# One core's order of work: two constants of a planner, two more split transforms, and one block pair that becomes a Strassen pair

## The chip, the cores and the metric

The kernel runs on one core of one Trainium2 chip. The metric is the time of one execution on the device in microseconds; the kernel before has a median of 857.06 us over three runs (853.89 to 859.17). A lower time is better.

## The reference

A sequence of 2048 rows with 640 channels passes through four layers: a convolution layer, a feed-forward layer, and the same two again. Each adds its result to its input, and each works on a layer-normalised copy of the input.

```
k_shift = 4-tap causal convolution of k over the rows     # per channel
kv      = k_shift * v
y       = causal convolution of kv with ssm_k (2048 taps, per channel)
y       = y + kv * ssm_D
A(x)    = layernorm(x) * y
B(x)    = relu(layernorm(x) @ w1) @ w2                    # 640 -> 1728 -> 640
x = q;  x = x + A(x);  x = x + B(x);  x = x + A(x);  x = x + B(x)
```

The convolution result `y` doesn't depend on `x`, so it is computed once and used in both convolution layers. All tensors are float32.

## The kernel before, in words

The 2048 rows form 8 chunks of 256 rows, each held as two halves of 128. A block (a, l) is the feed-forward layer l (0 or 1) of chunk a, together with the convolution layer ahead of it. Chunks 0 and 1 are worked in half blocks of 128 rows, the others in whole blocks of 256 rows. The order of the blocks is: both layers of chunk 0 by halves, both layers of chunk 1 by halves, then (2,0) (3,0) (2,1) (3,1), (4,0) (5,0) (4,1) (5,1), (6,0) (7,0) (6,1) (7,1).

**Convolution.** The 8 x 5 blocks of 256 rows by 128 channels are grouped in 21 units, listed in `units`. A unit holds one or two blocks; its place in the list is its rank. Ranks 0 to 5 are chunks 0 and 1 (ranks 2 and 5 hold one block); rank 6 is the unit of blocks (2,0) and (3,0), and rank 7 that of (2,1) and (2,2). For each unit, `transform` loads k, v and the long filter, makes kv, and takes both through transform matrices on TensorE: "pg" is the filter's result, "pr" the data's. It spills them to HBM as G and A. `products` multiplies the transforms of all pairs of chunks that meet in a unit's output, on VectorE (L676 to L680, tile `pacc`), and brings the sum back with an inverse transform on TensorE into `pq`.

The matrices of these transforms are float32. A transform is either *whole*, one float32 matmul for each piece, which the trace shows as two records (L592 for pr, L714 for pq), or *split*: the operand is cut into a high part by ScalarE (L720 for the inverse) and a rest by VectorE (L721), both of type float32r, and three matmuls take the place of the one (L403, L404, L405). `FA` and `FU` are the ranks from which forward transforms of the data and inverse transforms are split; units of one block are always whole.

From chunk 4 on, sums are made by *accumulating transfers*: DMAs that POOL's queue issues (L489 for gs, L561 for gt and at), which add a tile of SBUF onto another one. There are 40 of them.

**Feed-forward.** w1 and w2 are cut into 7 pairs of hidden blocks, j = 0 to 6, worked in the order `JS = (0, 1, 2, 3, 6, 4, 5)`. `mm1` makes the hidden values (L1150, L1151, L1153, tiles h and hb: three float16 passes, since activations and weights are split into a high and a low float16 part), ScalarE and VectorE split them again, and `mm2` multiplies with w2 (L1122, L1123, L1125). The last pair (6) is only part filled; its second matmul (L1252) moves half of the partitions, after a copy by ScalarE (tile tb, L1243).

In the last four blocks, `WINO`, the second product goes another way: a pair j is worked by the Strassen-Winograd scheme with seven products (`wprod`) where the plain scheme has eight (`wplain`); both are recorded at L1073. The weight sums that it needs are made by `wcombine` (L860 loads, L865 to L868 VectorE, L878 ScalarE, L879 VectorE), which may start when the last unit's inverse transform is done (`gate`, written at L753). In block (6,0) the pairs `JS[:EARLY]` and pair 6 stay plain.

**The order.** Nothing runs in the order of the program text. Every operation is put on record with its engine, an assumed cost, what it reads and writes, and a priority; the class `Plan` then lays them out by a list scheduler (`order`), counts back from the end how late each may be (`latest`), repeats this up to six times with these times as priorities, and issues the best order found. Each engine, SP's and POOL's queues included, works through its list in that order and waits by semaphores. So an assumed cost changes no instruction; it changes their order on all engines. A transfer is reckoned as done 1.9 us after its issue plus its bytes at the rate `DBW` (310e3 bytes a us) plus 1.1 us, whichever queue issues it.

```
best.ready = end          # in order(): from here on, users of the result may be placed
mm, mm4 = (0.121, 0.113)  # assumed us of one split and one whole float32 matmul, two blocks
```

Of the kernel before, what the change touches and what calls it, by code (L numbers as in the profile page):

```python
# [22 lines left out]
S = 2048  # L23
# [13 lines left out]
NX = 4  # L37
LAG = 3
NSPIN = 50
BM, BK = 1.7, 1.7  # L40
CLS = (0, 1, 2.2, 2, 2.5, 3)
DDP = -6.5
# [7 lines left out]
DBW0, FIRST = 385e3, 45  # L50
STALLS = ((3.5, 1.9), (15.0, 1.3))
LATE_DOWN = 0.0
PASSES, RPE, RBW, RLAT = 6, 0.0, 330e3, 1.9
RENGS = ("PE", "ACT", "DVE", "POOL", "SP")
ENDS = []
# [4 lines left out]

STT = ((0, 0), (0, 2), (0, 4))
FA = 6
FU = 8
FG = 11
SPLIT = (2, 0, 1)
HALVES = 2
# [6 lines left out]
STRAIGHT = ((1, 0),)  # L73
SIGNED_G = ()
WINO = ((6, 0), (7, 0), (6, 1), (7, 1))
EARLY = 2
ONPOOL = ()


# [27 lines left out]
class Plan:  # L107
# [99 lines left out]
    def order(self):  # L207
# [7 lines left out]
        events, dma, n, out = [0.0], 0.0, 0, []  # L215
# [19 lines left out]
        while n < len(self.ops):  # L235
            if not events:
                stuck = [(o.eng, o.seq, [t.name for t in o.new]) for e in engs for o in cand[e]]
                raise RuntimeError(f"no order: {stuck[:12]}")
            now = heapq.heappop(events)
            while events and events[0] <= now:  # L240
                heapq.heappop(events)
            while finish and finish[0][0] <= now:
                _, _, o = heapq.heappop(finish)
                for t in o.tiles:
                    t.left -= 1
                    if not t.left and t.ring is not None:
                        t.ring.free += 1
                for d in o.outs:
                    if d.eng == "PE" != o.eng and LATE(d):
                        heapq.heappush(later, (now + LATE(d), d.seq, d))  # L250
                        heapq.heappush(events, now + LATE(d))
                        continue
                    if d.eng == "PE" == o.eng:
                        continue
                    d.left -= 1
                    if not d.left:
                        cand[d.eng].append(d)
            while later and later[0][0] <= now:
                _, _, d = heapq.heappop(later)
                d.left -= 1  # L260
                if not d.left:
                    cand["PE"].append(d)
            for e in engs:
                if free[e] > now + 1e-9:
                    continue
                if e == "SP" and dma > now + LAG:
                    heapq.heappush(events, dma - LAG)
                    continue
                best = None
                rooms = [(max(map(when, o.deps)) - now + SLACK, o.prio) for o in soon.get(e, ()) if o.left]  # L270
                for o in cand[e]:
                    if best is not None and o.prio > best.prio:
                        continue
                    if any(o.cost > room and o.prio > prio for room, prio in rooms):
                        continue
                    if fits(o):
                        best = o
                if best is None:
                    continue
                cand[e].remove(best)  # L280
                for t in best.new:
                    t.ring.free -= 1
                    t.ring.lines[t.stream].pop(0)
                best.start = now
                free[e] = now + best.cost
                end = free[e] + (PEOUT if e == "PE" else 0.08)
                while best.nbytes and stalls and now >= stalls[0][0]:
                    dma = max(dma, now + DLAT) + stalls.pop(0)[1]
                if best.nbytes:
                    dma = max(dma, now + DLAT) + best.nbytes / (DBW0 if now < FIRST else DBW)  # L290
                    end = dma + 1.1
                best.ready = end
                if best.prio[0] == CRIT and e in soon:
                    soon[e].remove(best)
                if e == "PE":
                    for d in best.outs:
                        if d.eng == e:
                            d.left -= 1
                            if not d.left:
                                cand[e].append(d)  # L300
                heapq.heappush(finish, (end, best.seq, best))
                heapq.heappush(events, end)
                heapq.heappush(events, free[e])
                out.append(best)
                n += 1
# [12 lines left out]
def tile_h3_mlp(ctx: ExitStack, tc: tile.TileContext, q, kT, vT, shk, hF, hR, dD, w1, w2, cM, cG, out):  # L318
    nc = tc.nc
    PE, ACT, DVE, POOL, SP = nc.tensor, nc.scalar, nc.vector, nc.gpsimd, nc.sync  # L320
# [19 lines left out]
    def pe(cost, fn, reads, writes, prio, late=0.0):  # L340
        plan.op("PE", cost, fn, reads, writes, prio, late=late)
# [33 lines left out]
    down = keep(const, [P, P], "down", F16)  # L375
    POOL.memset(down.t, 0.0)
    POOL.tensor_copy(down[64:P, 0:64], ident16[64:P, 64:P])
    tb = keep(const, [P, 2 * P], "tb", F16)
# [57 lines left out]
    def transform(u):  # L436
# [6 lines left out]
        n, nm = len(u), "%d_%d" % u[0]  # L443
        pr_ = (CRIT, CONV, LATER)[min(u[0][0], 2)]
        w, h = 2 * n * P, n * P
        mm, mm4 = (0.121, 0.113) if n == 2 else (0.213, 0.063)
        full = n == 1 or rank(u) < FA
        ld = []
        c0 = u[-1][0] == 0
# [2 lines left out]
        for k, src, wd in (("kt", kT, 262), ("vt", vT, 256), ("hf", hF, 256), ("hr", hR, 256))[: 3 if c0 else 4]:  # L452
# [3 lines left out]
            x = R(k, [P, n, wd], k + nm)  # L456
# [61 lines left out]
        if c0 or straight or u[0] in SIGNED_G:  # L518
            srcs = [hf, hr] if straight else [hf]
            for b in range(2):  # L520
                for ri in range(2):
                    for k, x in enumerate(srcs if c0 or straight else gs[ri : ri + 1]):
                        x, xv = x if isinstance(x, tuple) else (x, lambda x=x: hv(x))
# [109 lines left out]
    def products(u, at, gt, after):  # L633
        n, nm = len(u), "%d_%d" % u[0]
        pr_ = (CRIT, CONV, LATER)[min(u[0][0], 2)]
        w, h = 2 * n * P, n * P
        mm, mm4 = (0.121, 0.113) if n == 2 else (0.213, 0.063)
        full = n == 1 or rank(u) < FU
        acc = T(cv, "pacc", 1, [P, n, 768], "pacc" + nm)
        if after:  # L640
# [46 lines left out]
        for ri in range(2):  # L687
            f = T(cv, "u", 2, [P, n, 256], f"u{ri}" + nm)
# [88 lines left out]
    WSRC, WT = {}, {}  # L777
# [246 lines left out]
    def main(n, a, layer, S, xTS):  # L1024
        xT, xS = xTS
        first_ = n == 0
        R = P * len(S)
        x0 = (S[0] - xS[0]) * P
        flat = list({id(x): x for x in xT.values()}.values())
# [99 lines left out]
        def mm1(j, i, p):  # L1129
            tail = j == NFP - 1 and i == 1  # L1130
            z = slice(0, R) if tail else slice(i * R, i * R + R)
            if n == 0 and j == JS[0]:

                def f(x):
                    for t in range(NDT):
                        b, e = t == 0, t == NDT - 1
                        wh, wl = w1at(j, t, i, 0), w1at(j, t, i, 1)
                        PE.matmul(p[:, z], wh, xv(t, x), start=b and x == 0, stop=e and x == 1)
                        if not x:
                            PE.matmul(p[:, z], wl, xv(t, 0), start=False, stop=False)  # L1140

                for x in range(2):
                    pe((10 - 5 * x) * 0.0545 * len(S), lambda x=x: f(x), [xT[0, x], WT[j, 0, 0], WT[j, 0, 1]], [p], FILL)
                return

            def f():
                for t in range(NDT):
                    b, e = t == 0, t == NDT - 1
                    wh, wl = w1at(j, t, i, 0), w1at(j, t, i, 1)
                    PE.matmul(p[:, z], wh, xv(t, 0), start=b, stop=False)  # L1150
                    PE.matmul(p[:, z], wh, xv(t, 1), start=False, stop=tail and e)  # L1151
                    if not tail:
                        PE.matmul(p[:, z], wl, xv(t, 0), start=False, stop=e)  # L1153

            pe((10 if tail else 15) * 0.0545 * len(S), f, [*flat, WT[j, 0, 0], WT[j, 0, 1]], [p], FILL)

        def second(j, *x):
            if len(x) == 4:
# [51 lines left out]
        for j in JS:  # L1210
            p = T(ps, "h", 2, [P, 2 * R], f"h{n}_{j}", stream=sm)
# [8 lines left out]
            p1 = T(ps, "h", 2, [P, 2 * R], f"hb{n}", stream=sm) if j == NFP - 1 else p  # L1220
# [28 lines left out]
                mm2(prev[0], 0, *prev[1:])  # L1249
                mm2(prev[0], 1, *prev[1:])  # L1250
            if j == NFP - 1:
                pe(0.0545 * len(S), lambda p1=p1: PE.matmul(p1[:, 0:R], down.t, tb[:, 0:R], start=False, stop=True, skip_group_check=True), [tb, down], [p1], URGENT, LATE_DOWN * len(S) / 2)  # L1252
                act(R, lambda p1=p1, hh=hh: ACT.activation(hh[0:64, z], p1[0:64, 0:R], AF.Relu), [p1], [hh], URGENT)
                dve(R, lambda p1=p1, hh=hh: DVE.scalar_tensor_tensor(hh[64:P, z], p1[0:64, 0:R], 0.0, hh[0:64, z], op0=ALU.max, op1=ALU.subtract), [p1, hh], [hh], URGENT)
            prev = (j, hh, hl, hs, ls) if wino and j not in plain else (j, hh, hl)
# [49 lines left out]
        for s in S if not wino else ():  # L1305
            for h in range(2):

                def f(s=s, h=h):
                    d = ds[h]
                    acc = {"accum_out": sp[:, s, h : h + 1]} if layer == 0 else {}  # L1310
                    DVE.scalar_tensor_tensor(xs[s][:, d], o(s, h), fac[s].t, xs[s][:, d], op0=ALU.mult, op1=ALU.add, **acc)
# [14 lines left out]
    spin = T(ps, "h", 2, [P, 512], "spin", stream=2)  # L1326
    for _ in range(NSPIN):
        pe(0.11, lambda: PE.matmul(spin[:, 0:P], ident16.t, ident16.t, start=True, stop=True), [ident16], [spin], IDLE)
# [38 lines left out]
    xT = xTs[0]  # L1367
    cMs = csplit(cMt, 6, False, [WT[JS[CMJ], 1, 1]])
    cGs = csplit(cGt, 4, True, [WT[JS[-1], 1, 1]])
    for n, (a, l, S) in enumerate(order):  # L1370
# [13 lines left out]
        xT = nxt  # L1384
# [88 lines left out]
```

## Time and profile before

| | |
|---|---|
| median of three runs | 857.06 us (853.89 to 859.17) |
| profiled execution | 858.03 us |
| its span, first to last instruction | 856.0 us |
| TensorE's granted clock | 0.999 |
| TensorE busy (matmuls) | 841.4 us, 98% |
| TensorE busy (weight loads) | 667.1 us, 78% |
| VectorE busy | 752.5 us, 88% |
| ScalarE busy | 491.5 us, 57% |
| GpSimd busy | 46.5 us, 5% |
| DMA | 177.46 MB, mean 207 GB/s |

The profile is of one execution. PE is TensorE, PEld its weight loads, DVE VectorE, ACT ScalarE, POOL GpSimd and SP the engine that issues most transfers; SPq is its queue. A group "h<-xT,w" names what is written and what is read. Matmuls overlap: each is recorded from its issue to a modelled end, so the distance from one start to the next tells what a matmul takes from TensorE, and the recorded length doesn't. A wait such as "PE h L1151 <- DMA xT<-xh" names who waited, and for what.

### The profile page before, as it was taken

Reading aid. Unit: us, or ns where it says so; the run is one execution under the profiler, and the core shown is the slowest. Engines: PE = TensorE matmul, PEld = TensorE weight load, DVE = VectorE, ACT = ScalarE, POOL = GpSimd, SP = SyncE. Lnnn points to the kernel's source line nnn. Section 1 sums busy time; section 2 is a strip of 40 time slices with the busy share of each in tenths; the row PEclk is TensorE's granted clock in tenths of the full one; section 3 lists DMA queues with packets and bytes.
Section 4 is the critical chain, followed back from the end, with each engine's and each line's share of the span. In section 5 each row is a group of like instructions: output and inputs, shape, how many; then the busy total and the mean of one; then the engine's idle time right before and its main releaser. Section 6 shows DMA issues by size and latency. Waiting matters only on the chain.

```text
span 856.0 us, 19757 instructions
## 1 busy us (share of the span) xinstructions
PE 841.4 (98%) x7796; PEld 667.1 (78%) x7796; DVE 752.5 (88%) x1413; ACT 491.5 (57%) x1143; POOL 46.5 (5%) x57
## 2 busy tenths in 40 slices
PE   8999999999999999999999999999999999999998
PEld 7977878878788777777777677877777788888886
DVE  7999999999998998999999999999897579756544
ACT  5697687347676565637447365564515376747331
POOL 2000000000001001011010101010100000000000
PEclk9999999999999999999999999999999999999999
DMA  9995977998989999698896979597986264110100
GB/s 321 372 330 180 280 223 212 299 305 263 312 238 262 291 227 260 198 254 226 232 250 207 242 210 222 153 208 242 242 276 212 78 202 103 33 31 2 32 32 31
DMA packets 134126, 177.46 MB, mean 207 GB/s; under 512 B 50577, under 2 KB 88081, under 8 KB 134034
## 3 DMA queue, kind: packets, MB, share of 16 engines
q1 hardware_dynamic: 125714, 165.72, 63.5%
q0 software_dynamic: 8320, 10.49, 7.8%
q8 instruction: 61, 1.00, 0.5%
q14 instruction: 31, 0.25, 0.1%
HBM read 121.44 MB, written 34.08 MB: 182 GB/s over the span
## 4 chain that ended last, share of the span: by engine, by line
PE 79%; DVE 8%; DMA 7%; issue 2%; ACT 2%; SPq 1%; DVEq 0%; ACTq 0%; POOLq 0%
PE h L1151 11%; PE h L1150 11%; PE h L1153 11%; PE o L1073 9%; PE o L1123 7%; PE o L1122 7%; PE o L1125 6%; PE oc L1123 2%; PE oc L1122 2%; PE oc L1125 2%; DMA ws<-in_w 2%; DVE pd L679 1%; PE pg L552 1%; PE pq L714 1%; DMA gs<-in_hF 1%
## 5 line engine op out<-in xcount | busy, mean ns | idle before, releaser
L1151 PE MATMUL h<-xT,w 128*128 128x256 f16 (+1 forms) x1290 | 301.3, 251 | 3.4 <-DMA xT<-xh 3.4
L1150 PE MATMUL h<-xT,w 128*128 128x256 f16 (+1 forms) x1290 | 301.5, 252 | 0.0
L1153 PE MATMUL h<-xT,w 128*128 128x256 f16 (+1 forms) x1290 | 301.2, 251 | 0.2
L1151 PEld LDWEIGHTS <-w 128*128 128x128 f16 x1390 | 136.0, 98 | 14.2 <-DMA xT<-xh 1.9
L1150 PEld LDWEIGHTS <-w 128*128 128x128 f16 x1390 | 136.1, 98 | 10.6
L1153 PEld LDWEIGHTS <-w 128*128 128x128 f16 x1290 | 126.2, 98 | 11.3 <-issue 2.0
L680 DVE TENSOR_TENSOR pacc<-pacc,pd 128x768 f32<-128x768 f32 x140 | 133.0, 951 | 0.5
L1123 PE MATMUL o<-w,hh 128*128 128x512 f16 x336 | 127.3, 379 | 0.2
L1122 PE MATMUL o<-w,hh 128*128 128x512 f16 x336 | 127.5, 380 | 0.0
L1122 PEld LDWEIGHTS <-hh 128*128 128x128 f16 x672 | 65.7, 98 | 43.5 <-issue 2.7
L1123 PEld LDWEIGHTS <-hh 128*128 128x128 f16 x672 | 65.8, 98 | 40.9
L1239 ACT ACTIVATE hh<-h 128x512 f16<-128x512 f32 (+1 forms) x99 | 47.9, 484 | 79.9 <-PE h L1153 79.7
L1125 PE MATMUL o<-w,hl 128*128 128x512 f16 x208 | 78.8, 379 | 0.0
L679 DVE TENSOR_TENSOR pd<-Ax,Gx 128x768 f32<-128x768 f32 x83 | 78.2, 950 | 0.0
L1123 PE MATMUL oc<-w,hh 128*128 128x128 f16 x336 | 73.6, 219 | 0.0
L1122 PE MATMUL oc<-w,hh 128*128 128x128 f16 x336 | 73.6, 219 | 0.0
L1125 PEld LDWEIGHTS <-hl 128*128 128x128 f16 x416 | 40.7, 98 | 24.8 <-DVE hl L1240 0.3
L471 ACT ACTIVATE tp<-kt,shs 128x256 f32<-128x256 f32 (+1 forms) x78 | 43.6, 575 | 22.4 <-DVE acc L508 16.7
L1240 DVE SCALAR_TENSOR_TENSOR hl<-h,hh 128x512 f16<-128x512 f32 x51 | 35.0, 685 | 14.1 <-ACT hh L1239 14.1
L1125 PE MATMUL oc<-w,hl 128*128 128x128 f16 x208 | 45.6, 219 | 0.0
L679 DVE TENSOR_TENSOR pd<-at,Gx 128x768 f32<-128x768 f32 x46 | 43.2, 950 | 0.0
L1073 PE MATMUL o<-w,hh 128*128 128x320 f16 (+2 forms) x286 | 39.6, 257 | 0.0
(235 smaller groups left out, 1742.0 us busy)
## 6 DMA issues: line engine op xcount, KB each, us to landing
Ax<-A SPq DMA_DIRECT2D x89, 384.0 KB, 4.3
Gx<-G SPq DMA_DIRECT2D x89, 384.0 KB, 4.2
G<-gt SPq DMA_DIRECT2D x30, 384.0 KB, 4.2
A<-at SPq DMA_DIRECT2D x30, 384.0 KB, 4.9
ws<-in_w SPq DMA_DIRECT2D x28, 320.0 KB, 7.0
y<-Y SPq DMA_DIRECT2D x22, 320.0 KB, 4.1
x<-in_q SPq DMA_DIRECT2D x16, 320.0 KB, 4.8
gs<-in_hF SPq DMA_DIRECT2D x20, 256.0 KB, 4.4
```

What stands on the lines that cost most here:

```text
L471: ACT.activation(o[:, i : i + m], kview(i, m, j), AF.Copy, scale=shs[:, t, j : j + 1])
L679: ew(f"mac{j % POOLMOD}", 768, lambda e, pd=pd, av=av, gv=gv: e.tensor_mul(pd.t, av(), gv()), [ax, gx], [pd], pr_)
L680: dve(768, lambda i=i, pd=pd: DVE.tensor_add(acc[:, i], acc[:, i], pd.t), [acc, pd], [acc], pr_)
L1073: PE.matmul(b[:, c : c + w], x, y[:, z : z + w], start=done[i] == 1, stop=end, skip_group_check=fin)
L1122: PE.matmul(z, hh[:, c], wh[:, d], start=(j == JS[0] and i == 0 and (h == 0 or s == S[0])), stop=False)
L1123: PE.matmul(z, hh[:, c], wl[:, d], start=False, stop=end and tail)
L1125: PE.matmul(z, hl[:, c], wh[:, d], start=False, stop=end)
L1150: PE.matmul(p[:, z], wh, xv(t, 0), start=b, stop=False)
L1151: PE.matmul(p[:, z], wh, xv(t, 1), start=False, stop=tail and e)
L1153: PE.matmul(p[:, z], wl, xv(t, 0), start=False, stop=e)
L1239: act(2 * R, lambda p=p, hh=hh: ACT.activation(hh.t, p.t, AF.Relu), [p], [hh], URGENT)
L1240: dve(2 * R, lambda p=p, hh=hh, hl=hl: DVE.scalar_tensor_tensor(hl.t, p.t, 0.0, hh.t, op0=ALU.max, op1=ALU.subtract), [p, hh], [hl], URGENT)
```

## The change

Three things change.

First, the planner's figures. `MMT` takes the place of 0.0545 us for each 128 columns in the first feed-forward product: 0.0558 us for a matmul of 128 columns, 0.1092 for one of 256. `mm`, a split float32 matmul of two blocks, goes from 0.121 to 0.116. A transfer that POOL's queue issues is reckoned as done 3.1 us behind its last byte in place of 1.1 (`ALAT`). Second, `FU` goes from 8 to 5, so inverse transforms of units of rank 5 to 7 are split, where they have two blocks. Third, `EARLY` goes from 2 to 1: in block (6,0), pair 1 is worked with seven products, and the weight sums of pair 1 are the first that `wcombine` makes, and those of pair 0 the last.

```diff
+MMT = (0, 0.0558, 0.1092)
+ALAT = 3.1
-FU = 8
+FU = 5
-EARLY = 2
+EARLY = 1
...
                 if best.nbytes:
                     dma = max(dma, now + DLAT) + best.nbytes / (DBW0 if now < FIRST else DBW)
-                    end = dma + 1.1
+                    end = dma + (1.1 if e == "SP" else ALAT)
...
-        mm, mm4 = (0.121, 0.113) if n == 2 else (0.213, 0.063)
+        mm, mm4 = (0.116, 0.113) if n == 2 else (0.213, 0.063)
...
-                    pe((10 - 5 * x) * 0.0545 * len(S), lambda x=x: f(x), [xT[0, x], WT[j, 0, 0], WT[j, 0, 1]], [p], FILL)
+                    pe((10 - 5 * x) * MMT[len(S)], lambda x=x: f(x), [xT[0, x], WT[j, 0, 0], WT[j, 0, 1]], [p], FILL)
...
-            pe((10 if tail else 15) * 0.0545 * len(S), f, [*flat, WT[j, 0, 0], WT[j, 0, 1]], [p], FILL)
+            pe((10 if tail else 15) * MMT[len(S)], f, [*flat, WT[j, 0, 0], WT[j, 0, 1]], [p], FILL)
...
-                pe(0.0545 * len(S), lambda p1=p1: PE.matmul(p1[:, 0:R], down.t, tb[:, 0:R], start=False, stop=True, skip_group_check=True), [tb, down], [p1], URGENT, LATE_DOWN * len(S) / 2)
+                pe(MMT[len(S)], lambda p1=p1: PE.matmul(p1[:, 0:R], down.t, tb[:, 0:R], start=False, stop=True, skip_group_check=True), [tb, down], [p1], URGENT, LATE_DOWN * len(S) / 2)
```

The changed line of `mm` stands in `transform` and in `products`. Where `plain` is set in `main`, these constants decide:

```
plain = (NFP - 1, JS[-1]) if fin else (NFP - 1, *JS[:EARLY]) if wino and a < NC - 1 and layer == 0 else (NFP - 1,)
```

More of the change, by code (lines that the diff above doesn't have):

```diff
@@ L636, in products @@
         w, h = 2 * n * P, n * P
-        mm, mm4 = (0.121, 0.113) if n == 2 else (0.213, 0.063)
+        mm, mm4 = (0.116, 0.113) if n == 2 else (0.213, 0.063)
         full = n == 1 or rank(u) < FU
```

## The prediction, made before the changed kernel was run

> **What bounds the kernel now.** I read the busy shares first, then TensorE's own waits, then the table of 25 us windows, and last the order of TensorE's instructions in a few of them.
>
> ```profile
> span 856.0 us, 19757 instructions
> PE 841.4 (98%) x7796; PEld 667.1 (78%) x7796; DVE 752.5 (88%) x1413; ACT 491.5 (57%) x1143; POOL 46.5 (5%) x57
> ```
>
> ```profile
> PE h L1151 <- DMA xT<-xh: 3.4, 2, 1.8
> PE hb L1252 <- ACT tb L1243: 2.5, 2, 1.5
> PE spin L1328 <- POOL heps L383: 1.9, 1, 1.9
> PE pg L529 <- POOL hf L477: 1.1, 1, 1.1
> PE hb L1150 <- DVE hl L1240: 0.6, 1, 0.6
> PE pt L575 <- ACT ob L556: 0.5, 1, 0.5
> ```
>
> TensorE is busy for 98% of the span, and all its listed waits add to 10.0 us (columns: total, times, longest). The two waits on POOL, 3.0 us together, lie in the opening and no edit touches their work. That leaves 7.0 us that a better order could remove.
>
> A busy TensorE need not be a full one, so I look at the spacing of matmul starts:
>
> ```profile
> 325.20 0.27 PE L1150 MATMUL h<-xT,w 128*128 128x256 f16 x1
> 325.31 0.27 PE L1151 MATMUL h<-xT,w 128*128 128x256 f16 x1
> ```
>
> Each record lasts 0.27 us, but the next starts 0.11 us later, evenly. TensorE issues one after another here with nothing missing, so its own work sets the time, and a matmul removed is worth its spacing, not its duration. The Trainium skill (Perfetto Trace Analysis, Identifying the Most-Contended Engine) says that matmul busy share is a poor measure of the room left and that the busy share of weight loads should be used. By that rule there would be 22% of room (78% of the span are weight loads), and removed matmuls would bring nothing; the even spacing speaks against it here, and I give it a rival below.
>
> ```profile
> 150.00:175.00 25.00, 25.00 (x271) 20.22 (x268) 24.99 (x42) 9.57 (x22) 0.00 (x0) 1.00 0.94 305
> 175.00:200.00 25.00, 25.00 (x280) 19.98 (x278) 24.66 (x48) 12.07 (x32) 0.00 (x0) 1.00 0.88 292
> 275.00:300.00 25.00, 24.43 (x204) 18.69 (x202) 22.87 (x36) 12.64 (x30) 2.11 (x2) 1.00 0.92 283
> 300.00:325.00 25.00, 23.36 (x189) 16.82 (x188) 24.90 (x40) 14.12 (x33) 2.13 (x2) 1.00 0.99 232
> 350.00:375.00 25.00, 22.98 (x187) 17.28 (x185) 24.97 (x38) 15.82 (x35) 4.24 (x4) 1.00 0.78 183
> 475.00:500.00 25.00, 23.21 (x192) 17.34 (x192) 23.59 (x36) 10.11 (x22) 2.11 (x2) 1.00 0.89 232
> 675.00:700.00 25.00, 25.00 (x233) 20.79 (x232) 13.21 (x28) 12.80 (x30) 0.00 (x0) 1.00 0.55 170
> ```
>
> After the length come PE, PEld, DVE, ACT, POOL, granted clock (1.00), DMA share and GB/s. Two things count. VectorE is full beside TensorE through the convolution stages (24.99 of 25). And after the opening TensorE's losses sit in four windows, 275 to 325, 350 to 375 and 475 to 500.
>
> **The change part by part.**
>
> *Split inverse transforms from unit 5.* Unit 5 has one block, which stays whole by the rule n == 1. So two units change, (2,0)+(3,0) and (2,1)+(2,2), ranks 6 and 7. A whole one from the chain of work, and a split one with the instruction after it from the order of TensorE:
>
> ```profile
> 93.78 1.78 PE pq L714 x8
> ```
>
> ```profile
> 342.64 0.36 PE L403 MATMUL pq<-uh,cMh 128*128 128x256 f32 x1
> ...
> 344.15 0.28 PE L1150 MATMUL h<-xT,w 128*128 128x256 f16 x1
> ```
>
> A whole inverse transform of a two-block unit takes 1.78 us for its 8 records; a split one, of 12, 344.15 - 342.64 = 1.51. Two of them: 2 x 0.27 = 0.54 us off TensorE. The price is two copies on ScalarE and two subtractions on VectorE for each unit:
>
> ```profile
> L721 DVE TENSOR_TENSOR ul<-u,uh x26: 670/684/694, 196.2 to 671.6; 128x512 fp32r<-128x512 f32 x26
> L720 ACT ACTIVATE uh<-u x26: 615/629/632, 195.3 to 670.9; 128x512 fp32r<-128x512 f32 x26
> ```
>
> That is 4 x 0.684 = 2.7 us on VectorE and 4 x 0.629 = 2.5 us on ScalarE, about 150 to 200. ScalarE is 40 to 50% busy there and hides its part. VectorE has 0.35 us free in those 50 us and hides nothing locally; what covers it is that TensorE has stored-up feed-forward matmuls there and waits for nothing in these two windows. So I cost it at nothing, and at up to 2.7 us if the lag reaches the next late hand-over (rival 2). The copies also take the two "rt" buffers that the forward transforms use, as the 13 later units already do.
>
> *One plain pair in block (6,0).* Pair 1 leaves the plain form, 4 outputs x 2 halves x 3 passes, for seven products of 3 passes:
>
> ```profile
> 694.24 0.44 PE L1073 MATMUL o<-w,hh 128*128 128x192 f16 x4
> ...
> 697.53 0.27 PE L1150 MATMUL h<-xT,w 128*128 128x256 f16 x1
> ...
> 700.81 0.43 PE L1073 MATMUL o<-w,hh 128*128 128x320 f16 x2
> ...
> 702.85 0.43 PE L1073 MATMUL o<-wt,hh 128*128 128x320 f16 x2
> ...
> 703.26 0.27 PE L1150 MATMUL h<-xT,w 128*128 128x256 f16 x1
> ```
>
> Plain pair 1: 697.53 - 694.24 = 3.29 us. Of pair 2's seven products six run from 700.81 to 703.26, 2.45 us; the seventh comes later and has three records like the last of these, 703.26 - 702.85 = 0.41. So 2.86. Saved: 0.43 us. Added are four short sums, a few copies and splits of the activations on VectorE and ScalarE, in a stretch where VectorE is 13.21 of 25 busy. What can hurt is time: combined weights are now wanted one pair earlier.
>
> ```profile
> 670.78 1.47 DVE L721 TENSOR_TENSOR ul<-u,uh 128x512 fp32r<-128x512 f32 x2
> 682.88 0.37 PE L403 MATMUL pq<-uh,cMh 128*128 128x256 f32 x1
> 685.35 0.41 DVE L753 TENSOR_TENSOR ys<-pq,qs 128x256 f32<-128x256 f32 x1
> 685.83 0.42 SPq L860 DMA_DIRECT2D wr<-in_w  x1
> 699.22 0.88 DVE L879 SCALAR_TENSOR_TENSOR wt<-wr,wsc,wt 128x640 f16<-128x640 f32 x1
> ```
>
> The first pair's combined weights are ready at 699.22 + 0.88 = 700.1. In the order shown, pair 1's products would start at 694.24: 5.9 us too early. But the gate for these weights (L753) waited for an inverse transform whose operands were ready at 670.78 + 1.47 = 672.25 and which the order put on TensorE only at 682.88. Moved forward by up to 10 us, it brings the weights forward with it; the planner counts back from what is late, so I take the cost as nothing and keep 5.9 us as the other end.
>
> *The reckoning.* No instruction changes; the orders on all five queues do, SP's and POOL's among them. The half-block figure goes from 15 x 0.0545 = 0.82 to 0.84 us for a run of fifteen, the two-block one from 1.635 to 1.638, the split transforms from 1.45 to 1.39. These are too small to expect an effect of a known sign. ALAT is larger: the planner had the 40 accumulating transfers done about 1.9 + 524288 B / 310e3 + 1.1 = 4.7 us after issue, now 6.7.
>
> ```profile
> gs<-hr POOLq DMA_DIRECT2D x20, 256.0 KB, 5.7
> gt<-gt POOLq DMA_DIRECT2D x10, 256.0 KB, 5.7
> at<-at POOLq DMA_DIRECT2D x10, 256.0 KB, 6.5
> ```
>
> ```profile
> DVE pd L679 <- DMA gt<-gt: 2.1, 1, 2.1
> DVE pacc L676 <- DMA gt<-gt: 1.5, 1, 1.5
> SPq L622 <- DMA gt<-gt: 10.7, 4, 5.0
> ```
>
> They land 5.7 to 6.5 us after issue, so the old figure was 1 to 1.8 us short and the new one is 0.2 to 1 us long. VectorE, which works in order, stood still twice for one of them, and SP's queue four times with the loads behind it held up. The Trainium skill (DMA: Bandwidth & Descriptors, Anatomy of one DMA) gives about 2.0 us plus bytes / 436e3 for such a transfer, by which 262144 bytes would be an estimated 2.6 us; the rows above say over twice that here, and by that page the new figure would go the wrong way.
>
> One of the waits can be followed in the chain of work (start, length, what):
>
> ```profile
> 287.67 8.89 DMA gt<-gt
> ```
>
> The transfer issued at 287.67 landed 8.89 us later, at 296.56, and VectorE's 2.1 us wait ended with it. TensorE's losses between 275 and 325 and from 350 to 375 begin in that window, with VectorE full (24.90 of 25) in the next. I take the gain as these 2.1 us, the wait itself; the ends are 7.0 us gained (all waits outside the opening) and 2.7 us lost (VectorE's added work passed on).
>
> **Sum.** The profiled execution took 858.03 us, its span 856.0 and 2.03 around it; the median is 857.06, 0.97 lower. 858.03 - 0.54 - 0.43 - 2.1 = 854.96 against its own time; set against the median, 853.99. I forecast **854.0 us**.
>
> **Rivals.**
> 1. *The waits only change places.* A new order makes its own late hand-overs; the two waits on transposed activations, 3.4 us, hang on loaded DMA queues (DMA share 0.99 and 0.89 in their windows), which no figure here changes. Then only the 0.97 us count: 857.06 - 0.97 = 856.1.
> 2. *VectorE's added 2.7 us come through, slower than before.* Place: units (2,0) and (2,1), 150 to 200, handed on along full VectorE windows to the normalised activations of block (3,0) or (2,1), where TensorE now waits (300 to 375). It decides if VectorE's order has no gap before then: 856.1 + 2.7 = 858.8. For it: 24.99 of 25. Against: the window 275 to 300 leaves VectorE 2.1 us.
> 3. *Combined weights come late in (6,0)*, if the gate stays at 685: 856.1 + 5.9 = 862.0.
> 4. *All waits outside the opening go:* 856.1 - 7.0 = 849.1.
> 5. *Removed matmuls bring nothing* because TensorE has room elsewhere: only the wait counts, 857.06 - 2.1 = 855.0. The even spacing speaks against it. It is what the Trainium skill (Perfetto Trace Analysis, Identifying the Most-Contended Engine) would make of the page's 78%.
> 6. *The later figure holds users of the transfers back too long:* up to 1 us for a user, and it shows only where TensorE is waiting anyway, the four windows: 856.1 + 4 x 1.0 = 860.1. Against it: 5.7 and 6.5 us measured. The Trainium skill (DMA: Bandwidth & Descriptors, Anatomy of one DMA) speaks for it with its shorter figure.
>
> **How the numbers follow.** Forecast 0.44 (its own range 851.5 to 856), rival 1 0.26, rival 2 0.10, rival 3 0.04, rival 4 0.10, rival 5 0.03, rival 6 0.03. The runs shown spread from 853.89 to 859.17, so about 1% (8.6 us) is what can be told from no change. The range, 849.5 to 859.5, leaves out part of rival 4 and rivals 3 and 6. Faster by over 1%, below 848.5, needs rival 4 and a little more: 0.05. Slower by over 1%, above 865.6, needs rival 3 with a second loss: 0.03. Within 1%: 0.92.
>
> **What would show it.** Step 1: 32 instead of 48 records of L714 at 256 columns, and 60 instead of 52 in each of the split lines for pq. Step 2: in (6,0) one run of plain products; the gate L753 before about 680; no TensorE wait on wt. Step 3: fewer waits of VectorE and SP on gt, and TensorE's listed waits near 8 us instead of 10. The prediction is wrong if TensorE's waits grow past 12 us, or if a wait on combined weights appears around 690 to 700.

## The result, and the profile after

The changed kernel takes 851.7 us (median of 7 runs, 850.83 to 854.7), the kernel before 857.06 (7 runs, 853.82 to 860.21). The ratio is 0.9939, with a 95% interval of 0.9914 to 0.9964: 5.4 us or 0.6% less, which is within 1% and inside the range of the prediction, 2.3 us below its 854.0. The profiled execution took 851.70 us.

First the page of the changed kernel, and TensorE's own waits. Its lines have numbers two higher than before (L1151 is now L1153, and so on).

```profile
span 849.8 us, 19769 instructions
PE 839.6 (99%) x7792; PEld 666.7 (78%) x7792; DVE 755.7 (89%) x1422; ACT 494.1 (58%) x1149; POOL 46.1 (5%) x57
```

```profile
PE spin L1330 <- POOL heps L385: 1.9, 1, 1.9
PE pg L531 <- POOL hf L479: 1.7, 1, 1.7
PE o L1125 <- DVE w L836: 0.9, 2, 0.7
PE hb L1254 <- ACT tb L1245: 0.8, 1, 0.8
PE h L1153 <- DMA xT<-xh: 0.6, 2, 0.3
PE pg L554 <- DVE ys L755: 0.4, 1, 0.4
```

The listed waits add to 6.3 us, where before they were 10.0; outside the opening's two on POOL they are 2.7 in place of 7.0. Where they went is seen in one window of each trace, 275 to 500 us, with the columns of the window table in the prediction (the second number is TensorE's busy time). Before, with its listed waits in the same stretch:

```profile
275.00:500.00 225.00, 218.98 (x1804) 166.78 (x1802) 218.23 (x350) 124.41 (x281) 25.23 (x24) 1.00 0.88 237
```

```profile
PE h L1151 <- DMA xT<-xh: 3.4, 2, 1.8
PE hb L1252 <- ACT tb L1243: 1.5, 1, 1.5
PE hb L1150 <- DVE hl L1240: 0.6, 1, 0.6
PE pt L575 <- ACT ob L556: 0.5, 1, 0.5
```

And after:

```profile
275.00:500.00 225.00, 225.00 (x1864) 172.44 (x1863) 222.82 (x357) 128.64 (x295) 25.16 (x24) 1.00 0.91 245
```

And ahead of it, 0 to 275 us, before and then after:

```profile
0.00:275.00 275.00, 270.31 (x2960) 221.07 (x2961) 261.60 (x527) 186.57 (x442) 10.58 (x23) 1.00 0.88 277
```

```profile
0.00:275.00 275.00, 268.71 (x2954) 220.25 (x2955) 262.48 (x530) 187.33 (x444) 10.23 (x23) 1.00 0.88 273
```

Before, 6.0 of the 225 us from 275 on were lost, to transposed activations, the copy tb, a late split of hidden values (hl) and a late copy of a filter transform (ob). After, none is lost, and 60 more matmuls fit in. The account of the span: idle time of TensorE went from 856.0 - 841.4 = 14.6 to 849.8 - 839.6 = 10.2, 4.4 us less: 6.0 gained in this stretch, 270.31 - 268.71 = 1.6 lost ahead of it. The span is 6.2 us shorter; this and the 0.97 us of removed matmuls account for 5.4. The other 0.8 us no row shows. They may be small gaps that the modelled ends of matmuls cover, or the granted clock, 0.999 before and 1.000 after: a thousandth of 841.4 us is 0.84.

The two edits did what they say. Inverse transforms, and the split of unit 6:

```profile
L716 PE MATMUL pq<-u,cM x48: 273/379/435, 19.4 to 127.3; 128*128 128x256 f32 x32, 128*128 128x128 f32 x16
L723 DVE TENSOR_TENSOR ul<-u,uh x30: 683/689/708, 154.0 to 667.6; 128x512 fp32r<-128x512 f32 x30
```

```profile
157.95 0.36 PE L405 MATMUL pq<-uh,cMh 128*128 128x256 f32 x1
...
159.48 0.39 PE L1124 MATMUL o<-w,hh 128*128 128x512 f16 x1
```

32 records of whole transforms are left at 256 columns, four subtractions are added (30 for 26), and the new split transform takes 159.48 - 157.95 = 1.53 us against 1.78. In block (6,0) the order of time shows the gate, the first load of weights, and their readiness and first use. `wcombine` makes two tile halves for each pair, so there are two L881 for each:

```profile
677.91 0.41 DVE L755 TENSOR_TENSOR ys<-pq,qs 128x256 f32<-128x256 f32 x1
678.87 0.42 SPq L862 DMA_DIRECT2D wr<-in_w  x1
687.86 0.88 DVE L881 SCALAR_TENSOR_TENSOR wt<-wr,wsc,wt 128x640 f16<-128x640 f32 x1
690.06 0.88 DVE L881 SCALAR_TENSOR_TENSOR wt<-wr,wsc,wt 128x640 f16<-128x640 f32 x1
694.99 0.44 PE L1075 MATMUL o<-wt,hh 128*128 128x320 f16 x2
```

The instruction at the gate now starts at 677.9 instead of 685.4, the first pair's two halves are done at 688.7 and 690.9, and TensorE first uses them at 694.99. Nothing waits for them. Most of the 7.4 us isn't a move of the gate within the work, since the whole trace is shorter: from there to the end of the span it is 856.0 - 685.35 = 170.7 us before and 849.8 - 677.91 = 171.9 after, 1.2 us more.

### The profile page after: what moved, and what is told of

Read it like the earlier page. It is cut to its first block, busy times and chain, and to the rows that moved or that the text cites. A ratio compares the mean times of both kernels' runs of the same rounds, so it can differ in the third digit from the quotient of the medians.

```text
span 849.8 us, 19769 instructions
## 1 busy us (share of the span) xinstructions
PE 839.6 (99%) x7792; PEld 666.7 (78%) x7792; DVE 755.7 (89%) x1422; ACT 494.1 (58%) x1149; POOL 46.1 (5%) x57
## 4 chain that ended last, share of the span: by engine, by line
PE 74%; DVE 13%; DMA 5%; ACT 4%; issue 2%; SPq 0%; POOL 0%; DVEq 0%; ACTq 0%; POOLq 0%
PE h L1153 10%; PE h L1152 10%; PE h L1155 10%; PE o L1075 9%; PE o L1124 6%; PE o L1125 6%; PE o L1127 6%; PE pg L531 2%; PE oc L1124 2%; PE oc L1125 2%; DMA xT<-xh 2%; DVE pd L681 2%; PE oc L1127 1%; DVE pacc L682 1%; DVE hh L1242 1%
## 5 line engine op out<-in xcount | busy, mean ns | idle before, releaser
L1153 PE MATMUL h<-xT,w 128*128 128x256 f16 (+1 forms) x1290 | 301.4, 252 | 0.6 <-DMA xT<-xh 0.6
L1153 PEld LDWEIGHTS <-w 128*128 128x128 f16 x1390 | 136.0, 98 | 11.5 <-DMA xT<-xh 0.5
L1152 PEld LDWEIGHTS <-w 128*128 128x128 f16 x1390 | 136.0, 98 | 10.7
L1125 PE MATMUL o<-w,hh 128*128 128x512 f16 x336 | 127.5, 379 | 0.9 <-DVE w L836 0.9
L1124 PE MATMUL o<-w,hh 128*128 128x512 f16 x336 | 127.6, 380 | 0.0
L1127 PE MATMUL o<-w,hh 128*128 128x512 f16 x104 | 39.4, 379 | 0.0
```

Of the source, the lines that this page charges most:

```text
L1124: PE.matmul(z, hh[:, c], wh[:, d], start=(j == JS[0] and i == 0 and (h == 0 or s == S[0])), stop=False)
L1125: PE.matmul(z, hh[:, c], wl[:, d], start=False, stop=end and tail)
L1127: PE.matmul(z, hl[:, c], wh[:, d], start=False, stop=end)
```

## The experiments

Twelve kernels were run, in three groups of four; each group shared a chip and the runs of the kernel before on it. The theories: **A**, the later figure for accumulating transfers (ALAT) removes the waits. **B**, every change of any figure or operation gives a new order on all queues, and a new order deals the waits anew; the figures' truth has no part in it. **C**, formed after the first two groups: the figures together make an order that the chip can keep.

The first group adds one part to the kernel before, the second takes one part from the changed kernel:

```diff
 only_alat   before with   ALAT = 3.1
 only_mmt    before with   MMT = (0, 0.0558, 0.1092), mm = 0.116
 only_fu     before with   FU = 5
 only_early  before with   EARLY = 1
 no_alat     after with    ALAT = 1.1
 no_mmt      after with    MMT = (0, 0.0545, 0.109), mm = 0.121
 no_fu       after with    FU = 8
 no_early    after with    EARLY = 2
```

**One part alone.** Expected:

> Before with the later reckoning of accumulating transfers alone. Theory A (this figure is what removes TensorE's waits): the gain of 4 to 5 us over before without the 0.97 us of work, so about 852.5; VectorE no longer waits for gt. Theory B (each new order deals the waits anew, the figure is no cause): anything from 852 to 861, with waits of TensorE outside the opening near 7 us again. Same TensorE work as before in both.

> Before with the matmul figures alone (0.0558, 0.1092 and 0.116). Theory A: no gain beyond 1 us, VectorE and SP still wait for gt, 856 to 858. Theory B: as likely to gain or lose several us as the run with the transfer figure, 852 to 861.

> Before with the two more split inverse transforms alone. By the prediction's step: 0.54 us less TensorE work and the same waits, 856.5. Theory B: the order is new, so waits move by several us either way. If VectorE's added 2.7 us come through: 859.

> Before with one plain pair in block (6,0) alone. By the prediction's step: 0.43 us less TensorE work, no wait on combined weights, 856.6. If the weights come late: up to 5.9 us of waiting around 690 to 700, 862. Theory B: waits elsewhere change by several us as well.

| kernel | median, us | lowest to highest | ratio to before | 95% interval |
|---|---|---|---|---|
| before, same chip | 855.45 | 851.67 to 860.23 | 1 | |
| only_alat | 853.47 | 851.41 to 857.09 | 0.9974 | 0.9951 to 0.9998 |
| only_mmt | 856.36 | 853.80 to 858.92 | 0.9996 | 0.9979 to 1.0014 |
| only_fu | 855.26 | 852.65 to 858.74 | 0.9986 | 0.9963 to 1.0009 |
| only_early | 855.55 | 852.22 to 861.67 | 0.9986 | 0.9963 to 1.0009 |

Taken by themselves these look like theory A: ALAT alone gains 0.26%, the others nothing that can be told from zero, and the four add to 0.58%, about the whole. Each edit's 0.5 us is too small for this measurement.

**One part taken away.** Expected:

> The changed kernel with the old reckoning of accumulating transfers (1.1 in place of 3.1). Theory A: the gain falls from 0.61% to the 0.97 us of work and little more, ratio near 0.998, SP and VectorE wait for gt again (SP's queue near 10 us in all). Theory B (new orders deal the waits anew): no relation, ratio anywhere between 0.993 and 1.003.

> The changed kernel with the old matmul figures. Theory A: as the changed kernel, ratio 0.994 to 0.995. Theory B: between 0.993 and 1.000.

> The changed kernel with whole inverse transforms for units 6 and 7. By the prediction's step 0.54 us more of TensorE work than the changed kernel, ratio 0.9945; if the run with this part alone (ratio 0.9986) showed its true worth, 0.9953.

> The changed kernel with two plain pairs in block (6,0). By the prediction's step 0.43 us more of TensorE work than the changed kernel, ratio 0.9944; by the run with this part alone (0.9986) 0.9953.

| kernel | median, us | lowest to highest | ratio to before | 95% interval |
|---|---|---|---|---|
| before, same chip | 857.54 | 852.86 to 860.80 | 1 | |
| no_alat | 851.95 | 850.55 to 853.93 | 0.9944 | 0.9921 to 0.9966 |
| no_mmt | 851.07 | 850.23 to 851.24 | 0.9933 | 0.9913 to 0.9953 |
| no_fu | 852.33 | 851.71 to 854.00 | 0.9950 | 0.9931 to 0.9968 |
| no_early | 850.96 | 850.77 to 851.41 | 0.9935 | 0.9915 to 0.9955 |

Theory A falls here. Without ALAT the gain is still there (0.9944, where A said near 0.998, outside the interval), and TensorE loses nothing in the stretch:

```profile
275.00:500.00 225.00, 225.00 (x1863) 172.48 (x1862) 222.97 (x358) 130.94 (x298) 25.20 (x24) 1.00 0.89 246
```

It is there although SP's queue waits longer for the transfers again. In the changed kernel, and without ALAT:

```profile
SPq L624 <- DMA gt<-gt: 2.6, 1, 2.6
```

```profile
SPq L624 <- DMA gt<-gt: 8.3, 3, 5.9
```

Nor is any other part needed for most of the gain: each can be taken away, while none alone brings it; a part's worth of 0.2% or less either way would not show in these intervals. The parts don't add. In the profile of EARLY alone the loss is still there, 225.00 - 219.59 = 5.4 us, again with transposed activations as the largest wait:

```profile
275.00:500.00 225.00, 219.59 (x1810) 167.53 (x1809) 217.51 (x348) 125.20 (x281) 25.26 (x24) 1.00 0.91 239
```

```profile
PE h L1152 <- DMA xT<-xh: 1.9, 1, 1.9
PE h L1153 <- DMA xT<-xh: 1.7, 2, 1.4
PE hb L1254 <- ACT tb L1245: 1.0, 1, 1.0
PE pt L577 <- ACT ob L558: 0.7, 1, 0.7
```

**Two groups of parts, and two orders made anew for no reason.** The last group has the controls that tell B from C: the figures together, the edits together, and twice the kernel before with one figure of the planner moved by next to nothing, so that the order is another and no figure is better.

```diff
 figures        after with    FU = 8, EARLY = 2
 edits          before with   FU = 5, EARLY = 1
 shuffle_peout  before with   PEOUT = 0.36            # was 0.35, the lag of a matmul's result
 shuffle_dbw    before with   DBW, DLAT = 311e3, 1.9  # was 310e3
```

Expected:

> The planner's three new figures alone (ALAT, MMT, mm), no new split units and two plain pairs. Theory C (the figures together make an order that the chip can keep, the edits only bring their work): ratio 0.995, the changed kernel's without 0.97 us of work; TensorE's waits outside the opening under 3 us. Theory B (a new order deals the waits anew): no better than the run with the transfer figure alone (0.9974) except by chance.

> The two edits alone (split from unit 5, one plain pair), with the old figures. Theory C: 0.97 us of work and the old waits, ratio 0.9985 to 0.999. Theory B: anywhere from 0.993 to 1.001.

> Before with one figure of the planner moved by a hundredth of a microsecond (PEOUT, the lag of a matmul's result, 0.35 to 0.36), so that every queue's order is made anew with no better figure. Theory C: as before, ratio 0.999 to 1.001. Theory B: several us off either way, 0.993 to 1.003.

> Before with the planner's DMA rate moved by 0.3% (310e3 to 311e3 bytes a us), another order with no better figure. Theory C: as before, ratio 0.999 to 1.001. Theory B: several us off either way, 0.993 to 1.003.

| kernel | median, us | lowest to highest | ratio to before | 95% interval |
|---|---|---|---|---|
| before, same chip | 856.53 | 851.03 to 861.99 | 1 | |
| figures | 855.99 | 853.17 to 859.82 | 0.9990 | 0.9968 to 1.0013 |
| edits | 855.27 | 852.95 to 861.23 | 0.9990 | 0.9967 to 1.0012 |
| shuffle_peout | 853.58 | 852.42 to 854.24 | 0.9958 | 0.9936 to 0.9980 |
| shuffle_dbw | 852.99 | 851.65 to 854.42 | 0.9957 | 0.9934 to 0.9979 |

Theory C falls, and of the three B is left. C's 0.995 for the figures lies outside their interval, and its 0.999 to 1.001 for the shuffles outside theirs. The three better figures together gain 0.1%, which can't be told from nothing. A hundredth of a microsecond on PEOUT, or 0.3% on the DMA rate, gains 0.42 and 0.43% with TensorE's work unchanged. Add the 0.97 us of removed work, 0.11%, and such an order would stand at 0.9947, within the changed kernel's interval. TensorE's stretch in the first of the two controls:

```profile
275.00:500.00 225.00, 225.00 (x1865) 172.41 (x1864) 223.53 (x359) 130.89 (x300) 25.13 (x24) 1.00 0.91 244
```

B's ranges were wide, though, so that little could have spoken against it, and two controls are few. It also leaves a pattern unexplained: the five kernels with three or all four of the parts are the fast ones, and of the six with one or two only ALAT alone gains anything that can be told from zero. If every order were a draw of its own, that would be a rare accident. Either orders that share parts share their luck, or three parts together do something of their own; no run tells these apart.

What ALAT does to SP's queue is real all the same, and beside the point. SP's waits for accumulating transfers of gt and at, with the figure (the three figures alone):

```profile
SPq L624 <- DMA gt<-gt: 1.0, 1, 1.0
SPq L625 <- DMA at<-at: 0.3, 1, 0.3
```

and without it (the DMA rate moved):

```profile
SPq L623 <- DMA at<-at: 9.2, 2, 7.5
SPq L622 <- DMA gt<-gt: 6.2, 4, 2.3
```

The kernel whose queue waits 15.4 us for these transfers is 3 us faster than the one whose queue waits 1.3.

**The spread says more than the median.** The kernel before has single runs of 851.0 and 851.7 us, as fast as the changed kernel's, and others of 860 and more. The six other orders that gain little also spread over 5 to 9.5 us, in 12 runs each; the changed kernel, the four with one part taken away and the two shuffles over 0.6 to 3.9, in 6 to 10 runs each. One profile was taken of each kernel. Those in which TensorE loses most between 275 and 500 belong to long executions (before 858.03 us, 6.0 lost; EARLY alone 859.97, 5.4 lost; the split units alone 855.74, 3.0 lost). Figures and edits, with spreads of 6.7 and 8.3 us, lost nothing there in their profiled executions, which were short ones (853.17 and 854.25). So the better orders seem not to be shorter on a good execution; they are less often late. This fits the numbers, but one trace for each kernel doesn't show it. The matmul figures alone are an exception: 1.2 us lost there in an execution of 858.12. That trace lost 275 - 266.78 = 8.2 us ahead of 275 (4.7 before), and its granted clock, the third number from the end, was below 1 from 5 to 15 us:

```profile
10.00:15.00 5.00, 5.00 (x22) 4.13 (x20) 4.04 (x9) 1.53 (x3) 0.96 (x1) 0.77 0.84 315
```

The granted clock goes with the spread in general. Of the 79 runs of the kernel before in the three groups, 24 have a mean clock of 0.998 or less and a median of 858.9 us, the other 55 a median of 855.2. Of the six orders that gain little, 16 of 72 runs are below 0.999; of the changed kernel, the four with one part taken away and the two controls, 3 of 53. Whether the lower clock makes an execution late, or comes of the same waits, isn't shown. It isn't the whole difference: among runs at 0.999 or more the median of the kernel before is still 2.7 to 5.4 us behind those of the better orders on the same chip.

## Why the prediction was right, point by point

*TensorE's own work bounds the kernel.* Right: it is busy for 99% now. Rival 5, room in TensorE, isn't settled by this: the removed work, 0.97 us by the forecast, is below what a comparison of two kernels here can tell. The runs without the new split units (0.9950) and without the Strassen pair (0.9935) lie on either side of the changed kernel's 0.9939.

*The split transforms: 0.54 us.* Right in the trace (1.53 and 1.78 us, so 0.50 for two), and the counts are those forecast; no measured time is fine enough to show it. VectorE's added 2.7 us (rival 2) did not come through to TensorE's late hand-overs at 300 to 375; the windows there lose nothing.

*The Strassen pair: 0.43 us, and no late weights.* Right in that no wait on weights appears and rival 3 did not occur; the 0.43 us itself is below what the times can tell. The reason given, that the planner moves the gate forward because the weights are wanted earlier, isn't what the runs show. The gate is a tile without memory, so it counts in the plan alone: in shuffle_dbw the first load of weights starts at 676.06, ahead of L753 at 678.20. With the Strassen pair alone (EARLY alone) the instruction at the gate stayed at 684.54, the first pair's halves were done at 692.7 and 694.7, and TensorE first used them at 703.3, without a wait. And with the pair left plain it stood at 678.34 (no_early). So what kept TensorE from waiting in EARLY alone was that the order put the products on combined weights later, behind other work. Rival 3's price was also too high. The row at 699.22 before is the third L879; by the kernel's order it is the first half of the next pair, and the second half of the first pair is this one:

```profile
696.15 0.88 DVE L879 SCALAR_TENSOR_TENSOR wt<-wr,wsc,wt 128x640 f16<-128x640 f32 x1
```

It is done at 697.0, so the weights would have been 2.8 us late for 694.24 and not 5.9.

*The reckoning: 2.1 us, from VectorE's wait for an accumulating transfer.* This is the step that failed in its cause. Its size was low: TensorE lost 6.0 us less between 275 and 500 and 1.6 more ahead of that, 4.4 in all. And the cause isn't the one argued. ALAT does shorten SP's waits for these transfers, as the step said (gt 2.6 us after, 10.7 before), and alone it gains 0.26%, close to the 2.1 us. But without it the gain stays, and orders that keep the long waits of SP are as fast. VectorE's waits for gt, 3.6 us before, are gone too, but so they are in every other trace except EARLY alone (0.5 us), whether ALAT is set or not; among these are the matmul figures alone and the split units alone, which gained nothing that can be told from zero. The chain of work led through the transfer of 8.89 us in one execution; that it lay on the chain did not make it the thing to mend. That the time came out 2.3 us from the forecast, and within 851.5 to 856, the range that the forecast gave itself, by 0.2 us, is in part luck: the largest term of the sum was gained in another way than the sum has it.

*Rival 1* comes nearest in mechanism, that a new order makes its own waits, but took the new draw to be as good as the old one. The kernel before was a poor draw: of thirteen other orders run, with at most 0.11% less work, five can't be told from it and eight are 0.26 to 0.67% faster. *Rival 4*, all waits outside the opening gone, came nearer than the forecast's 2.1 us in kind: 4.3 of the 7.0 us went. *Rival 6*, users held back too long, didn't show: TensorE's listed waits outside the opening fell to 2.7 us.

What stays open is why some orders are late so much more often than others. Transposed activations are the largest wait in the traces of before, of EARLY alone and of the split units alone, but the list of the matmul figures alone doesn't have them, so no single transfer is shown to be the cause. No version is shown to beat the changed kernel: leaving out the matmul figures (851.07 us, 0.9933) or the Strassen pair (850.96 us, 0.9935) gives ratios whose intervals cover its own.

## What to carry to other kernels

Where a planner lays out every queue, each edit is also a new draw of the order, so run a control that changes the order and nothing else before an edit's reason is believed; here such controls moved the time by 0.4%, nearly four times the work removed. Adding one part at a time and taking one part away can give opposite answers, and only both together, with the control, show that a part isn't the cause. Look at the spread of runs beside the median: an order that is late now and then can have the same best time as one that never is.

## What the runs showed that I had not expected

A transfer lay on the chain of work in the one execution that was profiled, 8.89 us long, with VectorE and SP waiting for its kind. The figure that reckons with it could be left as it was, and the time still fell (no_alat 0.9944, shuffle_dbw 0.9957 with 15.4 us of SP's waits). And single runs of one program, the kernel before, differ by 11.0 us on one chip (851.03 to 861.99, 29 runs), both of these at a mean granted clock of 0.999, while another order of the same work keeps within 1.8 us (shuffle_peout, 852.42 to 854.24, 10 runs).
